# A gated mix of linear attention and a gated FFN: the first loads cut finer, and one transposed weight turned in two parts

## The chip, the cores and the metric

The kernel runs on one core of one Trainium2 chip. The metric is the device time of one execution in microseconds (us), lower being better; times of several executions are given by their median.

## The reference, cut to what matters

```
x = A_x                                   # [1, 2048, 640], bf16
g = sigmoid((x * gate_w).sum(-1))         # one gate for each token

# A: linear attention, H = 32 heads of Dh = 20
q, k, v = split(x @ wqkv)                 # wqkv [640, 1920]: columns q, k, v
pq = q @ w_phi (by head);  pk = k @ w_phi (by head)          # w_phi [32, 20, 20]
phi_q = [softmax(pq), softmax(-pq)];  phi_k = [softmax(pk), softmax(-pk)]
kv = phi_k^T v (by head, over all tokens);  z = sum of phi_k over tokens
o = (phi_q kv) / (phi_q z + 1e-6)
a = o @ wo

# B: gated FFN, F = 1728
b = (gelu(x @ w_gate) * (x @ w_up)) @ w_down

out = g * a + (1 - g) * b
```

## The kernel before, in words

The 2048 tokens are 16 tiles of 128 (`NT = 16`), in four blocks of four (`TB = 4`). The width D = 640 is five row blocks of 128 (`KD = 5`). `run` emits three parts in order: `loads`, `attention_state`, `ffn`. There is no loop on the chip: every instruction is written out by Python, and each engine runs its own in the order in which they were emitted. The small class `_Sched` keeps a semaphore for each engine and lanes of semaphores for each DMA queue; `sc.op` and `sc.dma` put a wait before an instruction for whatever wrote or still reads the buffers that it names. A buffer's key is the unit of such a wait: with the key `"wkT"` a reader waits for the whole tensor.

**Loads.** DMAs are issued on two queues, SyncE's (`"sp"`) and ScalarE's (`"act"`). The first x block is loaded as it lies, tokens on partitions, into `xtok`: two tiles on SyncE, two on ScalarE (`xload`, line 216). TensorE turns these four tiles itself (`x_transpose`, line 290), and VectorE (line 298) or ScalarE (line 296) copies the result to `xT`. ScalarE's queue then loads `w_phi` (line 229) and the gate vector (line 234); SyncE's loads the five row blocks of v's weight into `w3` (line 233, key `("wv", kt)`). After that SyncE issues transposing DMAs, in this order: x tiles 4 and 5, `wkT` (k's weight turned, line 220, one DMA for all five row blocks), x tiles 6 and 7, `wqT`, x tiles 8 to 11, x tiles 12 to 15 (x: line 224). The FFN's weights follow.

**State.** `attention_state` writes its order out by hand. TensorE begins with seven matmuls on a tensor of zeros (`warm(7)`, line 540), which VectorE fills first (line 536). Then come the four transposes of x, the v projection of tiles 0 to 3, row block by row block (`v_step`, line 363), and, interleaved, v projections of tiles 4 to 7 (`v_early`), the folds of `w_phi` into k's and q's weight (`fold`, line 331: row block kt of `wkT` or `wqT` times the block-diagonal `BD`, evacuated to `w3` or `wq2`), and k projections of tiles 0 to 3 (`k_early`, evacuated by exponentials on ScalarE, lines 413 and 416). The fragment of that order which later text refers to:

```
f(0,"k") f(1,"k") v_early(6) f(2,"k") f(3,"k") f(4,"k") v_early(7) k_early(0)
f(0,"q") f(1,"q") k_early(1) f(2,"q") f(3,"q") k_early(2) f(4,"q") k_early(3)
pq(0,1,1) pq(0,0,0) pq(0,3,3) gram(0) pq(0,2,2) ...
```

`pq(b, i, n)` computes one q feature block in PSUM bank 6 or 7 (by the parity of n); ScalarE reads it with two exponentials (line 518). `k_norm` normalises the k features on VectorE (lines 424, 428 and 433), and `gram` (line 449) adds phi_k^T v for one tile. All projections go through `mm`, whose matmul is line 351. Then the loop over tiles 4 to 15 repeats projection, normalisation, two `pq` and one `gram`.

**FFN.** `ffn` computes gate and up projections (line 351 again), the gelu (line 623) and the product (line 625), and the down projection together with the attention's output projection (line 708), block by block.

Of the kernel before, what the change touches and what calls it, by code (L numbers as in the profile page):

```python
# [3 lines left out]
P = 128  # L4
BF16 = mybir.dt.bfloat16
F32 = mybir.dt.float32
AF = mybir.ActivationFunctionType
# [100 lines left out]
class _Kernel:  # L108
    S, D, H, DH, F = 2048, 640, 32, 20, 1728
    KD = D // P  # L110
# [31 lines left out]
    def alloc(self):  # L142
        nc = self.nc
        S, D, KD, NT, BT, NFC, DH = self.S, self.D, self.KD, self.NT, self.BT, self.NFC, self.DH
        T = nc.alloc_sbuf_tensor
        self.xT = T("xT", [P, KD, S], BF16)
        self.wo_sb = T("wo_sb", [P, KD, D], BF16)
        self.wg_sb = T("wg_sb", [P, KD, 13 * P], BF16)
        self.wu_sb = T("wu_sb", [P, KD, 13 * P], BF16)
        self.wgu_sb = T("wgu_sb", [P, KD, P], BF16)  # L150
        self.wd_sb = T("wd_sb", [P, NFC, D], BF16)
        self.Eq = T("Eq", [P, 2, KD, S], BF16)
        self.KV = T("KV", [P, KD, 2, self.HB * self.DB], BF16)
        self.hmask = T("hmask", [P, 2, KD, self.HB], BF16)
        self.mask = T("mask", [P, KD, 8], BF16)
        self.ident = T("ident", [P, P], BF16)
        self.zero = T("zero", [P, 512], BF16)
        self.gz = T("gz", [P, P], BF16)
        self.gcol = T("gcol", [P, NT], F32)
        self.gtmp = T("gtmp", [P, NT], F32)  # L160
        self.Gm = T("Gm", [P, NT], F32)
        self.Gr = T("Gr", [P, NT], F32)
        self.BD = T("BD", [P, KD, 8 * DH], BF16)
        self.wphi_sb = T("wphi_sb", [P, KD, DH], BF16)

        def place(lists):
            size = {"b": 0}
            plans = []
            for items in lists:
                c = 0  # L170
                for name, shape, dt in items:
                    n = mybir.dt.size(dt)
                    for s_ in shape[1:]:
                        n *= s_
                    c = (c + 31) // 32 * 32
                    plans.append((name, shape, dt, c))
                    c += n
                size["b"] = max(size["b"], c)
            arena = T("arena%d" % len(self._arenas), [P, size["b"]], mybir.dt.uint8)
            self._arenas.append(arena)  # L180
            base = nc.lookup_mloc(arena).addr
            for name, shape, dt, c in plans:
                setattr(self, name, nc.alloc_sbuf_tensor_at(name, shape, dt, offset=base + c))
        self._arenas = []
        place([
            [("w3", [P, KD, 2 * D + 2], BF16), ("wq2", [P, KD, D], BF16)],
            [("hT0", [P, NFC, BT], BF16), ("gl", [P, 3, BT], BF16)],
        ])
        place([
            [("Ek", [P, self.NSE, 2, D], BF16), ("vaug", [P, self.NSV, self.H, self.DA], BF16),  # L190
             ("Dk", [P, self.NSE, 2, 2 * self.H], F32)],
            [("hT1", [P, NFC, BT], BF16)],
        ])
        place([
            [("xtok", [P, self.TB, D], BF16), ("wkT", [P, KD, D], BF16), ("wqT", [P, KD, D], BF16)],
            [("goT", [P, 8, KD, P], BF16), ("O1", [P, 2, D], BF16), ("O2", [P, 2, D], BF16),
             ("Og", [P, 2, D], BF16), ("RH", [P, 2, 8, 2, 16], F32), ("outsb", [P, 4, D], BF16)],
        ])
        self.ps = nc.alloc_psum_tensor("ps", [P, 4096], F32)
# [8 lines left out]
    def loads(self):  # L208
        sc, nc = self.sc, self.nc
        D, KD, DH, P_ = self.D, self.KD, self.DH, P  # L210
        w3 = self.wqkv.rearrange("(kt p) n -> p kt n", p=P)

        x4 = self.x[0:self.BT, :].rearrange("(p j) n -> p j n", j=self.TB)

        def xload(q, j):
            sc.dma(q, lambda e: e.dma_start(self.xtok[:, j:j + 2, :], x4[:, j:j + 2, :]),
                   writes=[("xtok", j), ("xtok", j + 1)])

        def wload(T, c0, key):
            sc.dma("sp", lambda e: e.dma_start_transpose(T[:, :, :], self.wqkv[:, c0:c0 + D]), writes=[key])  # L220

        def xturn(t, n):
            a, z = t * P, (t + n) * P
            sc.dma("sp", lambda e: e.dma_start_transpose(self.xT[:, :, a:z], self.x[a:z, :]),
                   writes=[("xT", k) for k in range(t, t + n)])
        sc.op("pool", lambda e: e.memset(self.gz[:, :], 0.0), writes=["gz"])
        xload("sp", 0)
        xload("act", 2)
        sc.dma("act", lambda e: e.dma_start(
            self.wphi_sb[:, :, :], self.wphi.rearrange("h d f -> (h d) f").rearrange("(i p) f -> p i f", p=P)),  # L230
            writes=["wphi"])
        for kt in range(KD):
            sc.dma("sp", lambda e: e.dma_start(self.w3[:, kt, 0:D], w3[:, kt, 2 * D:3 * D]), writes=[("wv", kt)])
        sc.dma("act", lambda e: e.dma_start(self.gz[0:KD, :], self.gw.rearrange("(k p) -> k p", p=P)), writes=["gz"])
        xturn(4, 2)
        wload(self.wkT, D, "wkT")
        xturn(6, 2)
        wload(self.wqT, 0, "wqT")
        xturn(8, 4)
        xturn(12, 4)  # L240
        half = 7 * P
# [10 lines left out]
        for r in (0, 1):  # L252
            sc.dma("sp", lambda e: e.dma_start(self.wd_sb[64 * r:64 * r + 64, 13, :], self.wd[13 * P:self.F, :]),
                   writes=[("wd13", r)])
        sc.dma("sp", lambda e: e.dma_start(self.wo_sb[:, :, :], self.wo.rearrange("(kt p) n -> p kt n", p=P)),
               writes=["wo"])
# [6 lines left out]
        for i in range(KD):  # L263
            n = self.HHI[i] - self.HLO[i] + 1
# [53 lines left out]
    def fold(self, kt, which, banks, ekey):  # L318
        sc = self.sc
        DH = self.DH  # L320
        wT = self.wkT if which == "k" else self.wqT
        for i in range(self.KD):
            lo, hi = self.HLO[i], self.HHI[i]
            for h in (0, 1):
                a, z = max(lo, 16 * h), min(hi, 16 * h + 15)
                if a > z:
                    continue
                n = (z - a + 1) * DH
                b, c0, k0 = banks[h], (a - 16 * h) * DH, (a - lo) * DH
                first, fin = (i == 0 or a == 16), (z in (15, 31) and i in (2, 4))  # L330
                sc.op("pe", lambda e: e.matmul(  # L331
                    self.bank(b)[:, c0:c0 + n], wT[:, i, kt * P:(kt + 1) * P], self.BD[:, i, k0:k0 + n],
                    start=first, stop=fin, skip_group_check=True),
                    reads=["w%sT" % which, ("BD", i)], writes=[("ps", b)], signal=fin)
        src = self.pair(banks)
        if which == "k":
            dst = self.w3[:, kt, self.D:2 * self.D].rearrange("p (b c) -> p b c", c=320)
        else:
            dst = self.wq2[:, kt, :].rearrange("p (i r c) -> p r i c", r=2, c=64)
            src = src.rearrange("p r (i c) -> p r i c", c=64)  # L340
        rd = [("ps", b) for b in banks]
        wr = [("w%s2" % which, kt)]
        if ekey == "d":
            self.sc.op("dve", lambda e: e.tensor_copy(dst, src), reads=rd, writes=wr)
        else:
            self.sc.op("act", lambda e: e.activation(dst, src, AF.Copy), reads=rd, writes=wr)
# [161 lines left out]
                      writes=[("KV", i, r, g)])  # L508
                self.kvk[i, r].append(("KV", i, r, g))

    def pq(self, b, i, n):
        sc = self.sc
        bank = 6 + n % 2
        for kt in range(self.KD):
            self.mm(bank, 0, 512, self.wq2[:, kt, i * P:(i + 1) * P], self.xT[:, kt, b * self.BT:(b + 1) * self.BT],
                    kt == 0, kt == self.KD - 1, [("xT", t) for t in range(4 * b, 4 * b + 4)] + [("wq2", kt)])
        for s, scale in ((0, 1.0), (1, -1.0)):
            sc.op("act", lambda e, s=s, scale=scale: e.activation(  # L518
                self.Eq[:, s, i, b * self.BT:(b + 1) * self.BT], self.bank(bank), AF.Exp, scale=scale),
                reads=[("ps", bank)], writes=[("Eq", b, s, i)])  # L520
# [11 lines left out]
    def attention_state(self):  # L532
        NT = self.NT
        order = [(b, i) for b in range(self.NB) for i in range(self.KD)]
        sc = self.sc
        sc.op("dve", lambda e: e.memset(self.zero[:, :], 0.0), writes=["zero"])

        def warm(n):
            for i in range(n):
                sc.op("pe", lambda e: e.matmul(self.bank(0), self.zero[:, 0:P], self.zero[:, :], start=True, stop=True),  # L540
                      reads=["zero"], writes=[("ps", 0)])
        vs, ve, xt = self.v_step, self.v_first_evac, self.x_transpose
        warm(7)
        xt(0, 6, "d")
        xt(1, 7, "a")
        xt(2, 2, "d")
        xt(3, 3, "a")
        for t in range(4):
            vs(t, 0)
        for t in range(4):  # L550
# [33 lines left out]
        self.k_norm(1)  # L584
        self.pq(0, 1, 1)
        self.pq(0, 0, 0)
        self.pq(0, 3, 3)
        self.columns = True
        self.gram(0)
        self.k_norm(2)  # L590
# [2 lines left out]
        n = 4  # L593
# [47 lines left out]
    def num(self, t):  # L641
        sc = self.sc
        NBK = self.NUMB
        DB, DH = self.DB, self.DH
        old = [("xtok", k) for k in range(4)] + ["wkT", "wqT"]
        w = self.HB * DB
        for i in range(self.KD):
            for s in (0, 1):
                for r in (0, 1):
                    bk, a, o0 = NBK + 2 * r + s, 64 * r, 3 * i * DB  # L650
# [4 lines left out]
                        signal=(i == self.KD - 1))  # L655
# [183 lines left out]
```

The softmax here doesn't subtract the row's maximum and nothing guards it: scores larger than these inputs give would overflow.

## Time and profile before

| what | value |
|---|---|
| median of 4 runs | 289.34 us (289.03 to 289.74) |
| profiled execution, time | 289.25 us |
| profiled execution, span | 288.0 us |
| TensorE busy (matmul) | 281.5 us, 98% of the span |
| TensorE weight loads | 190.0 us, 66% |
| VectorE busy | 166.7 us, 58% |
| ScalarE busy | 105.0 us, 36% |
| GpSimd busy | 27.6 us, 10% |
| issue to landing: `wkT`, `wqT` | 6.7 us, 8.6 us |
| issue to landing: v's row blocks, median of five | 4.7 us |
| ScalarE's table load | 1.28 us, from 2.46 us |

All times of the profile are counted from the start of the span; the execution takes 1.25 us more than the span. "PE" is TensorE's matmuls and "PEld" its weight loads, which run beside matmuls; DVE is VectorE, ACT is ScalarE, POOL is GpSimd, SPq is SyncE's queue of DMA issues. In the chain of waits each row is a start, a length and what the end of the kernel waited for during it. In a timeline each row is a start, a length, an engine, a line, an operation, and out<-in; a bracket at its end is the idle time before it and what ended that.

### The profile page before, as it was taken

How to read it: one execution, taken by the hardware profiler on the slowest of the kernel's cores; microseconds unless marked ns; L12 is line 12 of the kernel's file. 1: busy time of each engine (PE TensorE's matmuls, PEld its weight loads, DVE VectorE, ACT ScalarE, POOL GpSimd, SP SyncE). 2: the span in 40 equal slices, each digit the busy share in tenths (PEclk: the TensorE clock that was granted, in tenths of full speed). 3: DMA queues.
4: the chain of work that ended last, by engine and by line, in shares of the span. 5: the costliest groups of instructions: out<-in, count | busy, mean ns of one | idle time of the engine just before them, and what ended most of it. 6: DMA issues, size and time to landing. Idle time of an engine off the chain costs nothing.

```text
span 288.0 us, 7020 instructions
## 1 busy us (share of the span) xinstructions
PE 281.5 (98%) x3016; PEld 190.0 (66%) x3032; DVE 166.7 (58%) x337; ACT 105.0 (36%) x199; POOL 27.6 (10%) x52
## 2 busy tenths in 40 slices
PE   7999999999999999999999999999999999999996
PEld 3576689999994444444699744457764444777785
DVE  2248999999977552777776533227644232674001
ACT  3367887677663222222111332221133222022111
POOL 7000000000000000111113200001230000113000
PEclk9999999999999999999999999999999999999999
DMA  8999995000002000011112110000212000031211
GB/s 225 207 190 238 365 367 175 0 2 2 0 2 48 0 0 0 3 36 30 25 29 72 35 58 0 3 0 19 76 25 68 0 2 0 3 93 25 71 49 49
DMA packets 36938, 18.68 MB, mean 65 GB/s; under 512 B 28970, under 2 KB 36394, under 8 KB 36906
## 3 DMA queue, kind: packets, MB, share of 16 engines
q1 hardware_dynamic: 36096, 17.86, 24.7%
q8 instruction: 24, 0.39, 0.6%
q10 hardware_dynamic: 810, 0.35, 0.5%
q14 instruction: 8, 0.07, 0.1%
HBM read 9.04 MB, written 2.62 MB: 40 GB/s over the span
## 4 chain that ended last, share of the span: by engine, by line
PE 96%; DMA 1%; ACT 1%; issue 1%; ACTq 0%
PE ps L351 60%; PE ps L708 28%; PE ps L651 2%; PE ps L363 2%; PE ps L449 2%; DMA xtok<-in_A_x_dram 1%; PE ps L331 1%; ACT Ek L413 0%; PE ps L290 0%; ACT Eq L518 0%; ACT gl L631 0%; ACT outsb L721 0%; ACT gcol L416 0%; PE ps L313 0%; ACTq L42 0%
## 5 line engine op out<-in xcount | busy, mean ns | idle before, releaser
L625 DVE TENSOR_TENSOR hT<-ps,gl 128x512 bf16<-128x512 f32 x52 | 35.7, 690 | 55.2 <-PE ps L351 54.9
L708 PE MATMUL ps<-wd_sb,hT 64*128 64x320 bf16 (+2 forms) x918 | 67.5, 288 | 0.0
L351 PE MATMUL ps<-xT,wu_sb 128*128 128x512 bf16 (+1 forms) x266 | 64.0, 379 | 0.2
L351 PE MATMUL ps<-xT,wg_sb 128*128 128x512 bf16 (+1 forms) x261 | 62.9, 379 | 1.2 <-issue 1.0
L623 ACT ACTIVATE gl<-ps 128x512 bf16<-128x512 f32 x52 | 30.9, 597 | 71.5 <-PE ps L351 64.9
L708 PEld LDWEIGHTS ps<-wd_sb,hT 64*128 64x128 bf16 x918 | 46.6, 94 | 12.5 <-ACT gl L623 0.8
L351 PEld LDWEIGHTS ps<-xT,wu_sb 128*128 128x128 bf16 (+1 forms) x270 | 26.5, 99 | 29.7 <-DVE hT L625 0.4
L680 POOL TENSOR_TENSOR Og<-O,O 128x640 bf16<-128x640 bf16 x16 | 22.3, 1393 | 236.7 <-DVE O L678 236.7
L351 PEld LDWEIGHTS ps<-xT,wg_sb 128*128 128x128 bf16 (+1 forms) x270 | 25.9, 99 | 28.7 <-issue 0.5
L721 ACT ACTIVATE outsb<-ps,Gm 128x320 bf16<-128x320 f32 (+2 forms) x31 | 14.6, 515 | 74.8 <-PE ps L708 74.8
L351 PE MATMUL ps<-w,xT 128*64 128x512 bf16 (+6 forms) x398 | 41.6, 325 | 0.2
L351 PEld LDWEIGHTS ps<-w,xT 128*64 128x64 bf16 (+1 forms) x400 | 35.8, 107 | 4.8
L708 PE MATMUL ps<-wo_sb,goT 64*128 64x320 bf16 (+2 forms) x340 | 28.1, 288 | 0.0
L351 PE MATMUL ps<-xT,wq 128*64 128x512 bf16 (+1 forms) x184 | 26.1, 380 | 0.4 <-ACT Eq L518 0.3
L433 DVE TENSOR_TENSOR Ek<-Ek,Dk 128x640 bf16<-128x640 bf16 x32 | 25.0, 821 | 0.6
L678 DVE TENSOR_TENSOR O<-ps,RH 128x640 bf16<-128x640 f32 x32 | 24.7, 815 | 0.0
L424 DVE TENSOR_REDUCE Dk<-Ek 128x64 f32<-128x1280 bf16 x16 | 23.7, 1478 | 0.2 <-ACT gcol L416 0.2
L518 ACT ACTIVATE Eq<-ps 128x512 bf16<-128x512 f32 x40 | 21.7, 604 | 1.1 <-PE ps L351 0.8
L413 ACT ACTIVATE Ek<-ps 128x640 bf16<-128x640 f32 x32 | 20.7, 702 | 3.5 <-PE ps L351 3.5
L708 PEld LDWEIGHTS ps<-wo_sb,goT 64*128 64x128 bf16 x340 | 17.9, 94 | 4.5
L351 PEld LDWEIGHTS ps<-xT,wq 128*64 128x64 bf16 (+1 forms) x185 | 15.3, 108 | 3.5 <-ACT Eq L518 0.8
L667 DVE RECIPROCAL RH<-ps 128x32 f32<-128x32 f32 x16 | 5.7, 358 | 18.3 <-PE ps L651 18.2
(65 smaller groups left out, 148.8 us busy)
## 6 DMA issues: line engine op xcount, KB each, us to landing
out_dram<-outsb SPq DMA_DIRECT2D x7, 320.0 KB, 2.4
wd_sb<-in_B_w_down_dram SPq DMA_DIRECT2D x1, 2080.0 KB, 14.0
wg_sb<-in_B_w_gate_dram SPq DMA_DIRECT2D x1, 1120.0 KB, 6.1
wu_sb<-in_B_w_up_dram SPq DMA_DIRECT2D x1, 1120.0 KB, 8.6
wg_sb<-in_B_w_gate_dram SPq DMA_DIRECT2D x1, 960.0 KB, 9.6
wu_sb<-in_B_w_up_dram SPq DMA_DIRECT2D x1, 960.0 KB, 10.2
w<-in_A_wqkv_dram SPq DMA_DIRECT2D x5, 160.0 KB, 4.7
wo_sb<-in_A_wo_dram SPq DMA_DIRECT2D x1, 800.0 KB, 9.7
```

Of the source, the lines that this page charges most:

```text
L351: self.sc.op("pe", lambda e: e.matmul(self.ps[a:z, bank * 512 + c0:bank * 512 + c0 + n], lhs[:, a:z], rhs, start=first, stop=fin), reads=r ...
L363: sc.op("pe", lambda e, c0=c0, n=n, bk=bk, col=col: e.matmul(self.bank(bk)[:, col:col + n], self.xT[:, kt, t * P:(t + 1) * P], self.w3[:, ...
L413: self.sc.op("act", lambda e, s=s, scale=scale: e.activation(self.Ek[:, se, s, :], self.ps[:, o:o + self.D], AF.Exp, scale=scale), reads=[ ...
L424: sc.op("dve", lambda e: e.tensor_reduce(self.Dk[:, se, 0, :].rearrange("p (s h) -> p s h", h=H), self.Ek[:, se, :, :].rearrange("p s (h d ...
L433: sc.op("dve", lambda e, v=v, r=r: e.tensor_tensor(v, v, r, ALU.mult), reads=[("Rk", se)], writes=[("Ek", se, s)])
L518: sc.op("act", lambda e, s=s, scale=scale: e.activation(self.Eq[:, s, i, b * self.BT:(b + 1) * self.BT], self.bank(bank), AF.Exp, scale=sc ...
L623: sc.op("act", lambda e: e.activation(self.gl[:, slot, :], self.bank(banks[0]), AF.Gelu_apprx_tanh), reads=[("ps", banks[0])], writes=[("g ...
L625: sc.op("dve", lambda e: e.tensor_tensor(hT[:, c, :], self.bank(banks[1]), self.gl[:, slot, :], ALU.mult), reads=[("ps", banks[1]), ("gl", ...
L678: dve(lambda e, o=o, f=f, s=s: e.tensor_tensor(o, V[s][:, :, :, 0:DH], f, ALU.mult), rb + [key(6 + s)], [("O", s, sl)], guard=old)
L680: sc.op("pool", lambda e: e.tensor_tensor(self.Og[:, sl, :], self.O1[:, sl, :], self.O2[:, sl, :], ALU.add), reads=[("O", 0, sl), ("O", 1, ...
L708: sc.op("pe", lambda e: e.matmul(self.bank(bk, w), lhs, rhs, start=opens and x == 0, stop=end and not opens, skip_group_check=True), reads ...
L721: sc.op("act", lambda e: e.activation(dst, self.bank(bk, w), AF.Copy, scale=g), reads=rd, writes=wr)
```

## The change

- The first x block is loaded by four DMAs of one tile each, all on SyncE's queue.
- The five row blocks of v's weight come behind them: blocks 0 and 2 on ScalarE's queue, 1, 3 and 4 on SyncE's. `w_phi` and the gate vector stay on ScalarE's queue, behind v's two blocks.
- ScalarE's first action is one exponential on a constant, which loads the function table. It writes a column of `gtmp`, which is used again only by `gates`, much later.
- `wkT` is turned by two DMAs, row blocks 0 and 1, then 2 to 4, with x tiles 6 and 7 between them. `wqT` remains one DMA. The keys of both are by row block now.
- The warm-up uses a constant tensor of ones that is there before the kernel begins, instead of zeros written by VectorE; six matmuls instead of seven.
- x tile 3 is evacuated by VectorE instead of ScalarE.
- The third `pq` of block 0 uses PSUM bank 0 instead of bank 7.

```diff
-        self.zero = T("zero", [P, 512], BF16)
...
         def xload(q, j):
-            sc.dma(q, lambda e: e.dma_start(self.xtok[:, j:j + 2, :], x4[:, j:j + 2, :]),
-                   writes=[("xtok", j), ("xtok", j + 1)])
-
-        def wload(T, c0, key):
-            sc.dma("sp", lambda e: e.dma_start_transpose(T[:, :, :], self.wqkv[:, c0:c0 + D]), writes=[key])
+            sc.dma(q, lambda e: e.dma_start(self.xtok[:, j, :], x4[:, j, :]), writes=[("xtok", j)])
+
+        def vload(q, kt):
+            sc.dma(q, lambda e: e.dma_start(self.w3[:, kt, 0:D], w3[:, kt, 2 * D:3 * D]), writes=[("wv", kt)])
+
+        def wload(T, c0, key, a, z):
+            sc.dma("sp", lambda e: e.dma_start_transpose(T[:, :, a * P:z * P], self.wqkv[a * P:z * P, c0:c0 + D]),
+                   writes=[(key, k) for k in range(a, z)])
...
         sc.op("pool", lambda e: e.memset(self.gz[:, :], 0.0), writes=["gz"])
-        xload("sp", 0)
-        xload("act", 2)
+        sc.op("act", lambda e: e.activation(self.gtmp[:, 0:1], self.nc.const_aps.tensor(1.0, [P, 1], BF16), AF.Exp),
+              writes=["gtmp"])
+        for j in range(self.TB):
+            xload("sp", j)
+        for kt in range(KD):
+            vload("act" if kt in (0, 2) else "sp", kt)
         sc.dma("act", lambda e: e.dma_start(
             self.wphi_sb[:, :, :], self.wphi.rearrange("h d f -> (h d) f").rearrange("(i p) f -> p i f", p=P)),
             writes=["wphi"])
-        for kt in range(KD):
-            sc.dma("sp", lambda e: e.dma_start(self.w3[:, kt, 0:D], w3[:, kt, 2 * D:3 * D]), writes=[("wv", kt)])
         sc.dma("act", lambda e: e.dma_start(self.gz[0:KD, :], self.gw.rearrange("(k p) -> k p", p=P)), writes=["gz"])
         xturn(4, 2)
-        wload(self.wkT, D, "wkT")
+        wload(self.wkT, D, "wkT", 0, 2)
         xturn(6, 2)
-        wload(self.wqT, 0, "wqT")
+        wload(self.wkT, D, "wkT", 2, 5)
+        wload(self.wqT, 0, "wqT", 0, 5)
         xturn(8, 4)
         xturn(12, 4)
...
-                    reads=["w%sT" % which, ("BD", i)], writes=[("ps", b)], signal=fin)
+                    reads=[("w%sT" % which, kt), ("BD", i)], writes=[("ps", b)], signal=fin)
...
-    def pq(self, b, i, n):
-        sc = self.sc
-        bank = 6 + n % 2
+    def pq(self, b, i, n, bank=None):
+        sc = self.sc
+        bank = 6 + n % 2 if bank is None else bank
...
-        sc.op("dve", lambda e: e.memset(self.zero[:, :], 0.0), writes=["zero"])
-
-        def warm(n):
-            for i in range(n):
-                sc.op("pe", lambda e: e.matmul(self.bank(0), self.zero[:, 0:P], self.zero[:, :], start=True, stop=True),
-                      reads=["zero"], writes=[("ps", 0)])
+        ones = self.nc.const_aps.tensor(1.0, [P, 512], BF16)
+        for i in range(6):
+            sc.op("pe", lambda e: e.matmul(self.bank(0), ones[:, 0:P], ones, start=True, stop=True), writes=[("ps", 0)])
         vs, ve, xt = self.v_step, self.v_first_evac, self.x_transpose
-        warm(7)
         xt(0, 6, "d")
         xt(1, 7, "a")
         xt(2, 2, "d")
-        xt(3, 3, "a")
+        xt(3, 3, "d")
...
-        self.pq(0, 3, 3)
+        self.pq(0, 3, 3, 0)
```

More of the change, by code (lines that the diff above doesn't have):

```diff
@@ L644, in num @@
         DB, DH = self.DB, self.DH
-        old = [("xtok", k) for k in range(4)] + ["wkT", "wqT"]
+        old = [("xtok", k) for k in range(4)] + [(w, k) for w in ("wkT", "wqT") for k in range(self.KD)]
         w = self.HB * DB
```

## The prediction

> **What bounds the kernel now.** I read the page first, then the chain of waits in order of time, then the first 30 us on TensorE, on SyncE's queue and on the DMA engines.
>
> ```profile
> PE 281.5 (98%) x3016; PEld 190.0 (66%) x3032; DVE 166.7 (58%) x337; ACT 105.0 (36%) x199; POOL 27.6 (10%) x52
> ...
> PE 96%; DMA 1%; ACT 1%; issue 1%; ACTq 0%
> ```
>
> TensorE is busy 98% and carries 96% of the chain, so a microsecond saved ahead of it counts only if everything that it reads later is there a microsecond sooner. The chain of waits has two places where TensorE waits for another:
>
> ```profile
> 0.80 4.12 DMA xtok<-in_A_x_dram
> ...
> 4.96 1.29 PE ps L290 x20
> 6.25 4.56 PE ps L363 x32
> ...
> 20.49 0.63 PE ps L331 x12
> ...
> 27.61 0.99 ACT Eq L518 x2
> 28.60 0.05 issue
> 28.65 1.25 PE ps L351 x5
> ```
>
> The first is the x block (to 4.96), the second a wait for ScalarE's exponentials of line 518, after which line 351 starts at 28.65; the timeline gives TensorE 0.34 us idle there. The change goes at both. Whether the first gain lives is read from what TensorE needs next. Its weight loads in time, and SyncE's issues of the transposing DMAs:
>
> ```profile
> 15.21 1.36 PEld L351 LDWEIGHTS ps<-w,xT 128*128 128x128 bf16 x10
> 16.53 0.97 PEld L331 LDWEIGHTS ps<-BD,wkT 128*128 128x128 bf16 x18
> 17.59 2.62 PEld L351 LDWEIGHTS ps<-w,xT 128*128 128x128 bf16 x20
> 20.22 0.72 PEld L331 LDWEIGHTS ps<-BD,wqT 128*128 128x128 bf16 x12
> ```
>
> ```profile
> 3.76 2.27 SPq L224 DMA_TRANSPOSE xT<-in_A_x_dram  x1
> 6.08 3.81 SPq L220 DMA_TRANSPOSE wkT<-in_A_wqkv_dram  x1
> 9.93 1.41 SPq L224 DMA_TRANSPOSE xT<-in_A_x_dram  x1
> 11.38 4.96 SPq L220 DMA_TRANSPOSE wqT<-in_A_wqkv_dram  x1
> 16.38 7.35 SPq L224 DMA_TRANSPOSE xT<-in_A_x_dram  x2
> ```
>
> The answers on the tiles give the time to landing: 5.5 us for x tiles 4 and 5 (9.3), 6.7 for wkT (12.8), 5.2 for x tiles 6 and 7 (15.1), 8.6 for wqT: 11.38 + 8.6 = 19.98. The first load from wqT is at 20.22, and after x landed TensorE began 0.05 later (4.92, 4.96). So wqT has **0.19 us to spare**; x tiles 6 and 7 have none (15.1 against 15.21). Are those transposes themselves full? The DMA rate in slices of 0.1 us, from 12 and from 16 us:
>
> ```profile
> GB/s 195 151 92 90 56 54 143 243 248 95 253 289 284 292 244 233 220 212 195 31 61 49 67 164 36 23 10 51 72 41 56 236 241 195 23 131 136 261 287 289
> GB/s 284 287 287 287 300 289 289 289 292 292 294 289 435 269 269 269 91 61 85 26 3 28 10 8 8 8 10 10 10 8 10 10 266 287 289 289 118 287 292 294
> ```
>
> They move 289 GB/s in a rush, then drop nearly to nothing, then rush again: once at each change from one transposing DMA to the next. Time lost is the length of a dip less its bytes over 289 GB/s: 0.11 us at 8.9 (into wkT), 0.89 from 11.4 (into x 6 and 7), 1.24 from 13.9 (into wqT), 1.47 from 17.6, 1.39 from 21.4. Mean of the five 1.02.
>
> **The change part by part.** *Front.* Now 2 x 320 KB land at 4.7 and 4.92. Four 160 KB loads on SyncE are issued 0.49 apart (row of line 233: five in 2.44). Bytes begin at about 2.0; one tile at some 380 GB/s (2.5 to 4 us) is 0.43, and landing follows the bytes by about 0.5. Tiles land near 3.1, 3.6, 4.1, 4.6; if ScalarE's two v rows share the engines at once, about 1.0 MB is ahead of the last, 2.0 + 2.65 + 0.5 = 5.15. Then five transposes (0.056 each, 20 weight loads in 1.12) and the v steps start at 5.0 to 5.5, not 6.09. The wait for the last copies goes too: 16 steps at the 0.273 of the last four (1.09) are 4.36, not 4.56. Front gain 0.8 to 1.3; I take 1.1.
>
> *Cost of the front.* ScalarE's table (1.28) is already hidden, at 2.46; first, it delays v row 0 between 0 (the queue runs on) and 1.28. Row 0 is then issued at 0.8 to 2.1, landing by 4.1 to 4.8 more (v rows): 4.9 to 6.9. At worst the v steps start 0.8 late. wphi moves behind two v rows: 3.1 + 4.3 = 7.4, five products of 0.30 on VectorE end at 9.0, with the gate column (10.9) and the v evacuations (11.38) queued behind them: hidden. The gate vector's landing is not shown; between wphi's 4.3 and wqT's 8.6 from an issue near 3.6 it is there at 7.9 to 12.2, against 10.58, so it costs 0 to 1.6 before cover; I take 0, as wphi is its neighbour. VectorE's memset (0.27) goes; tile 3's copy takes 0.49 on VectorE, not 0.70 on ScalarE. All of this is ahead of the wqT wait below and covered by it; without that cover it counts in full.
>
> *Warm-up.* Six matmuls without a wait, at 0.42 each, from about 0.9 end at 3.4, as tiles arrive. The seven of before start from 1.25 to 3.78, and at 4.96 the rate has doubled (the granted clock reads 1.00 in every window and doesn't show it; the spacing does). If it doubles later, 20 transposes lose 20 x 0.05 = 1.0: 0 to 1.0, covered likewise. I take 0.
> The Trainium skill, TensorE: Matmul & The Clock Gate, Part 1, asks for about 3.4 us of sustained work in a free-running window before full rate; six matmuls are less than that, and by the page alone the 1.0 would be due.
>
> *SyncE's queue.* Seven copies (four x, three v) stand before the first transpose, now six: it is issued up to 0.48 later, or at no cost if it waits for the v bytes anyway, which are the same in total. I take 0.24.
>
> *wk in two parts.* Same bytes, one transposing DMA more ahead of wqT, so one more dip: 0.11 to 1.47, taken at the mean, 1.02. Below nothing is possible too, if shorter DMAs overlap better; against it, x 6 and 7, the short one, has dips of 0.89 and 1.24 on its two sides.
> The Trainium skill, DMA: Bandwidth & Descriptors, Rules for kernel authors, says that transfers under 64 KB are mostly overhead; both parts of wk (320 and 480 KB) are above it, so by the page the split is near free and the sum would be the second rival's.
>
> x tiles 6 and 7 come earlier (two blocks ahead of them, not five), so the v step at 15.21 is freed. The second part of wk is wanted at 16.53, less the gain 15.4. From 9.3 by landing intervals (2.35 for two blocks, from wkT's 12.8 to 15.1) it lands at 9.3 + 2.35 + 2.35 + 2.6 = 16.6: part of the gain is lost there already. wqT decides.
>
> *Sum at the first q fold.* wqT lands 1.02 + 0.24 = 1.26 later, at 21.24; less the 0.19 to spare, TensorE is **1.07 later** than now, with the whole front gain turned into waits. Then *bank 0 for the third q product*: banks 0 and 1 are free after line 416 (27.6), so the 0.34 idle goes (low end 0.28, by ten matmuls of 0.216 from 26.21); the following gram needs VectorE's products at 29.30 and would start at about 29.45: free. Net 1.07 - 0.34 = +0.73. The profiled execution took 289.25 (span 288.0 and 1.25 around it), so 289.98; it lies 0.09 under the median 289.34. I say **290.0**.
>
> **The rivals.** *Faster: transposes keep up.* If smaller pieces overlap and wqT lands at 18.9 or earlier, TensorE never waits for it: -1.1 - 0.34 = -1.45, 287.9; between, each microsecond is one. It becomes faster by over 0.2% (0.58 us, about what a measurement of this kernel can tell from no change) once wqT lands 0.05 earlier than now. For it: the dip into wkT was 0.11. Against: the other four.
> *No difference: the extra dip is like that into wkT.* wqT lands between 0.05 earlier and 1.1 later, net -0.58 to +0.57: 288.7 to 289.9. The front gain is then hidden behind wqT and the 0.34 pays for the rest.
> *The front doesn't come early* (v rows and x share the same engines): v steps at 6.1; with wqT late as forecast it changes nothing, 290.0.
>
> **How the numbers follow.** Forecast case, wqT at least 1.1 later: 0.58 (0.10 of it for the third rival, which ends at the same time). No difference: 0.24. Faster: 0.18. Ends: the costs at 1.47 + 0.48 give 1.95 - 0.19 - 0.28 = +1.48, 290.7 to 290.8; I add 0.1 for the median. The low end reaches through the second rival into the first, 288.4, leaving out most of the first and little else. The likeliest case alone: 289.9 to 290.8.
>
> **What would show it.** Five transposing issues ahead of the x tiles 8 on, with five dips between 8 and 20 us; wqT landing near 21.2; TensorE idle for 1 to 2.5 us in all before line 331's folds; v steps from 5.0 to 5.5; no idle at line 518's wait. I am wrong if wqT lands at or before 20.0, or if TensorE's time after 30 us changes.

## The result, and the profile after

The changed kernel takes 290.72 us (median of 44 runs, 289.32 to 293.11), the kernel before beside it 289.45 (63 runs, 288.51 to 290.68). The ratio is 1.0052, with a 95% interval of 1.0041 to 1.0063: 1.5 us slower (1.2 to 1.8). The spread is as telling as the median: 3.8 us, against 2.2 before. The profiled execution took 292.68 (span 291.4) and so belongs to the long ones; it shows the loss enlarged, 3.4 us of span where the medians differ by 1.3.

The page has the same make-up as before, with 3.3 us more on TensorE for the same work (one matmul fewer):

```profile
PE 284.8 (98%) x3015; PEld 191.2 (66%) x3031; DVE 166.8 (57%) x337; ACT 104.5 (36%) x199; POOL 27.6 (9%) x52
...
PE 96%; DMA 2%; issue 1%; SPq 0%; ACT 0%
```

The chain of waits of the changed kernel (start, length, what the end waited for; lines are 5 higher than before in this part):

```profile
2.20 4.86 DMA xtok<-in_A_x_dram
7.05 0.05 issue
7.10 0.71 PE ps L295 x5
7.82 6.95 PE ps L368 x32
...
15.96 2.66 PE ps L356 x19
...
24.36 0.63 PE ps L336 x12
...
28.34 0.32 PE ps L336 x6
...
30.07 3.19 PE ps L356 x14
33.26 0.00 issue
33.26 0.46 PE ps L454 x11
```

The x block now holds the chain to 7.05, not 4.92. The 32 matmuls of the first v steps take 6.95, not 4.56. The first q fold stands at 24.36, 3.87 later than before's 20.49, and nothing waits for a transposed weight anywhere between. The idle time ahead of the third q product is gone: from the last q fold (28.34; before 24.48) to the first gram (33.26; before 29.90) it is 4.92 us, not 5.42, so **bank 0 gives 0.50**. What remains, 3.36, is the whole difference of the spans: after 33 us the two kernels run alike.

TensorE's weight loads in time show both losses (the bracket is the idle time before a row and what ended it):

```profile
3.78 0.45 PEld L295 LDWEIGHTS ps<-ident,xtok 128*128 128x128 bf16 x5 [1.13 <-DMA xtok<-in_A_x_dram]
4.52 0.45 PEld L295 LDWEIGHTS ps<-ident,xtok 128*128 128x128 bf16 x5 [0.29 <-DMA xtok<-in_A_x_dram]
5.61 0.45 PEld L295 LDWEIGHTS ps<-ident,xtok 128*128 128x128 bf16 x5 [0.64 <-DMA xtok<-in_A_x_dram]
7.10 0.45 PEld L295 LDWEIGHTS ps<-ident,xtok 128*128 128x128 bf16 x5 [1.03 <-DMA xtok<-in_A_x_dram]
...
12.28 0.29 PEld L368 LDWEIGHTS ps<-w,xT 128*128 128x128 bf16 x2 [0.25 <-issue]
12.81 1.62 PEld L368 LDWEIGHTS ps<-w,xT 128*128 128x128 bf16 x12 [0.25 <-issue]
```

Four waits, one for each tile of x: they land at 3.74, 4.48, 5.57 and 7.06 (the trace records sixteen landing events for a tile, its shares; it has landed with the last of them). And the weight loads of two v matmuls take 0.53 us (12.28 to 12.81) until 12.8, then 0.27: TensorE ran at half rate until then. The granted-clock view reads 1.00 for every stretch; the trace also keeps a record of changes of the clock, which that view doesn't show: it begins with full rate at 12.98 here and at 4.62 in the kernel before.

SyncE's queue stands as predicted, with five transposing DMAs ahead of the x tiles from 8 on:

```profile
4.10 2.04 SPq L226 DMA_TRANSPOSE xT<-in_A_x_dram  x1
6.19 2.58 SPq L221 DMA_TRANSPOSE wkT<-in_A_wqkv_dram  x1
8.81 1.41 SPq L226 DMA_TRANSPOSE xT<-in_A_x_dram  x1
10.26 2.08 SPq L221 DMA_TRANSPOSE wkT<-in_A_wqkv_dram  x1
12.38 4.59 SPq L221 DMA_TRANSPOSE wqT<-in_A_wqkv_dram  x1
```

wqT takes 8.2 us from there and lands at 20.6. That is 0.6 later than before, but TensorE reads it at 24.09, 3.5 after it is there.

Two theories came out of this. *Clock*: the shorter warm-up with gaps behind it keeps TensorE at half rate. *Transfers*: the last piece of the x block comes late because other loads share the engines with it. The prediction's own reason, wqT's landing after one more transposing DMA, is the rival.

### The profile page after: what moved, and what is told of

Its sections match the earlier page's. It is cut to its first block, busy times and chain, and to the rows that moved or that the text cites. A ratio compares the mean times of both kernels' runs of the same rounds, so it can differ in the third digit from the quotient of the medians.

```text
span 291.4 us, 7028 instructions
## 1 busy us (share of the span) xinstructions
PE 284.8 (98%) x3015; PEld 191.2 (66%) x3031; DVE 166.8 (57%) x337; ACT 104.5 (36%) x199; POOL 27.6 (9%) x52
## 4 chain that ended last, share of the span: by engine, by line
PE 96%; DMA 2%; issue 1%; SPq 0%; ACT 0%
PE ps L356 60%; PE ps L709 28%; PE ps L368 3%; PE ps L652 2%; PE ps L454 2%; DMA xtok<-in_A_x_dram 2%; PE ps L336 1%; SPq L215 0%; PE ps L295 0%; ACT gl L632 0%; ACT outsb L722 0%; PE ps L318 0%
```

## The experiments

Each ratio is against the kernel before, run beside it, with its 95% interval.

### The clock

**The warm-up filled up** (e1_fill). The changed kernel, with warm-up matmuls in the gaps between the transposes:

```diff
-        for i in range(6):
-            sc.op("pe", lambda e: e.matmul(self.bank(0), ones[:, 0:P], ones, start=True, stop=True), writes=[("ps", 0)])
...
+        warm(7)
         xt(0, 6, "d")
+        warm(1)
         xt(1, 7, "a")
+        warm(2)
         xt(2, 2, "d")
+        warm(4)
         xt(3, 3, "d")
```

> After, with more warm-up matmuls so that TensorE has work while x lands: 7 ahead of the first transpose, 1, 2 and 4 more between the four tiles' transposes (6, 0, 0, 0 in after). Theory clock: in after TensorE's idle gaps during the x loads (0.23, 0.38 and 0.77 us) keep it at half rate, in the profiled execution until about 13 us, and that is most of the loss. Then the v steps (32 matmuls, 6.95 us in the profile of after) take 4.4 to 4.8, the spread between runs shrinks, and the median falls from 290.7 to 289.5 to 290.0, x still landing at 7. Theory wqT (that of the prediction): TensorE waits for wqT in any case, so the median stays at 290.4 to 290.9.

Measured: 289.75 (289.28 to 290.11), ratio 1.0013 (1.0003 to 1.0022). The spread falls from 3.8 to 0.8. Its weight loads, and its chain:

```profile
5.61 0.28 PEld L295 LDWEIGHTS ps<-ident,xtok 128*128 128x128 bf16 x5 [0.43 <-DMA xtok<-in_A_x_dram]
```

```profile
7.15 0.45 PE ps L295 x5
7.60 4.37 PE ps L368 x32
...
21.56 0.63 PE ps L336 x12
```

The third tile's transposes start at 5.61 in both kernels; their loads take 0.28 here and 0.45 there, and the v steps 4.37 against 6.95. Full rate is on record from 4.85. Nothing else moved: x still lands at 7.1. So the clock is worth 0.97 us by the two medians (1.1 by the two ratios), 2.8 in the two profiled executions (the first q fold at 21.56 and 24.36). That 21.56 is 1.07 later than before's 20.49 with full rate early in both: the price of the late x block, read from one execution of each kernel.

**The warm-up alone** (e6_warm6_only). The kernel before, with six matmuls on the constant ones:

```diff
-        sc.op("dve", lambda e: e.memset(self.zero[:, :], 0.0), writes=["zero"])
+        ones = self.nc.const_aps.tensor(1.0, [P, 512], BF16)
...
-        warm(7)
+        warm(6)
```

> Before, with only the warm-up of after: six matmuls on a constant, from 0.84, ending at 3.4, and then 1.5 us of idle until x lands at 4.9. Theory clock: the rate doubles later in most runs, so the median is 0.4 to 1.5 us slower than before and the slowest run lies above 291. Rival: six are enough, or the gap does no harm; the median is that of before within 0.2 us. Starting 0.4 earlier could also gain up to 0.2.

Measured: 290.68 (289.62 to 291.23), ratio 1.0038 (1.0025 to 1.0051): 1.1 us slower (0.7 to 1.5) with nothing else touched; 1.46 by the two medians. Its chain:

```profile
4.73 2.32 PE ps L289 x20
7.05 5.33 PE ps L362 x32
```

The 20 transposes take 2.32, not 1.29, and the v steps 5.33, not 4.56; full rate came at 8.86. The six matmuls, from 0.84, end near 3.6 and TensorE then has nothing to do until x lands at 4.7.

The Trainium skill, TensorE: Matmul & The Clock Gate, Part 1, says that full rate comes after about 3.4 us of sustained work, watched in windows that run free of the kernel, so that one kernel differs from run to run. These runs agree in the scatter. With six matmuls and gaps the profiled execution got full rate at 12.98 (the change), at 8.86 (e6) and, in runs shown below, at 9.02 (e2) and 4.37 (e9). With seven or more it came between 4.62 and 6.05 (before, e1, e5, e7, e8, e10 to e12); e4, with the warm-up of before, has no such record, and its transposes ran at half rate. In e3, below, with six, it came at 3.65, after 2.7 us of matmuls, which is less than the page's 3.4; from there the record changes in steps of 3.41.

### The transfers

**w_phi behind the v rows** (e9_wphi_last).

```diff
-        sc.dma("act", lambda e: e.dma_start(
+        sc.dma("sp", lambda e: e.dma_start(
             self.wphi_sb[:, :, :], ...
```

> After, with w_phi's load (640 pieces of 40 bytes) moved from ScalarE's queue to SyncE's, behind x and v; v rows 0 and 2 stay on ScalarE's queue. Theory w_phi: its small pieces hold up the engines in the middle of x, and one engine above all (the last tile's sixteen shares land between 5.70 and 7.06 in after); without them the last tile lands at 5.0 to 5.7, and the median falls to 289.6 to 290.2. Theory v rows: the two v rows alone keep the last tile at 6.3 or later and the median at 290.4 to 291.0. The clock may still miss, so the spread stays about 2 us or more.

Measured: 290.05 (288.53 to 290.86), ratio 1.0013 (0.9995 to 1.0030). The last tile lands at 5.83 instead of 7.06. In the changed kernel w_phi's 640 pieces of 40 bytes, on ScalarE's queue, run from 4.47 us, among the last tile's bytes, and the last tile's sixteen shares arrive from 5.70 to 7.06; here from 5.28 to 5.83. The DMA queues from 4.5 to 5.0 us (packets, MB, time of the packets as a share of that of 16 engines, which can pass 100%; q1 is SyncE's queue, q10 ScalarE's), in the changed kernel and then here:

```profile
q10 hardware_dynamic: 586, 0.02, 80.4%
q1 hardware_dynamic: 78, 0.08, 50.8%
```

```profile
q1 hardware_dynamic: 164, 0.19, 110.5%
```

So in this half microsecond SyncE's queue, with x on it, moves 0.08 MB beside the small pieces and 0.19 without them. At the 380 GB/s of the prediction the missing 0.11 MB is 0.3 us (an estimate); the rest of the 1.2 goes with the uneven arrival of the shares (1.36 apart against 0.55), whose cause is not shown. The runs fall in two groups, 288.5 to 289.4 and 289.8 to 290.9, which fits the warm-up that is still the short one. The profiled execution is the shortest, with full rate from 4.37, and in it a weight has become late:

```profile
16.63 0.94 PEld L336 LDWEIGHTS ps<-BD,wkT 128*128 128x128 bf16 x18 [0.26 <-DMA wkT<-in_A_wqkv_dram]
```

**All v rows behind x, on SyncE's queue** (e2_v_behind).

```diff
-            vload("act" if kt in (0, 2) else "sp", kt)
+            vload("sp", kt)
```

> After, with all five v rows on SyncE behind the four x tiles, none on ScalarE. Theory sharing: in after the last x tile lands at 7.06 because the two v rows and w_phi on ScalarE's queue take the DMA engines at the same time; here it lands at 4.6 to 5.3 and the v steps start at 5.0 to 5.6 (7.6 in after); median 288.6 to 289.8. Rival, small loads: 160 KB tiles on one queue are slow by themselves; the last tile still lands after 6.3 and the median stays above 290.2. Theory wqT: x lands early, but TensorE then waits for wqT before line 336's q folds, which cannot start before 20.7; median 289.5 to 290.2.

Measured: 289.80 (288.97 to 290.83), ratio 1.0014 (0.9999 to 1.0028). The last tile lands at 6.07, between the two expectations: a miss of the experiment, for ScalarE's queue, freed of the v rows, now begins with w_phi, whose pieces run at 2.3 to 3.2. It takes a neighbour away and puts another one earlier. Full rate came at 9.02, so the time has the clock's loss in it too. The third tile landed at 5.68, and the fourth while the third was being turned:

```profile
5.73 0.99 PEld L295 LDWEIGHTS ps<-ident,xtok 128*128 128x128 bf16 x10 [1.24 <-DMA xtok<-in_A_x_dram]
```

**Single tiles in the kernel before** (e7_tiles_two_queues), on the two queues in turn (`xload` loads one tile), all else as before:

```diff
-        xload("sp", 0)
-        xload("act", 2)
+        xload("sp", 0)
+        xload("act", 1)
+        xload("sp", 2)
+        xload("act", 3)
```

> Before, with the x block in four loads of one tile, alternately on SyncE's and ScalarE's queue; nothing else moved. If loads of one tile are slow by themselves, the last tile lands after 5.3 (4.9 before) and the run is slower. If it is what shares the engines with them (v rows, w_phi's 640 pieces of 40 bytes), the last lands at 4.7 to 5.0, the first near 3.5, and the time is that of before within 0.3 us: the first tiles' transposes run earlier and fill the idle time, but the last tile sets the start of the v steps.

Measured: 289.71 (289.00 to 290.11), ratio 1.0012 (0.9999 to 1.0026). The last tile lands at 4.81, no earlier than the pairs do (4.59 to 4.92 in before, e4, e5, e6 and e8, which load them alike), and the next wait is there at once, for x tiles 6 and 7:

```profile
15.64 1.36 PEld L352 LDWEIGHTS ps<-w,xT 128*128 128x128 bf16 x10 [0.45 <-DMA xT<-in_A_x_dram]
```

### The parts by themselves

**wk in one part** (e3_wk_whole), in the changed kernel.

```diff
-        wload(self.wkT, D, "wkT", 0, 2)
+        wload(self.wkT, D, "wkT", 0, 5)
         xturn(6, 2)
-        wload(self.wkT, D, "wkT", 2, 5)
```

> After, with wkT turned by one DMA again, x tiles 6 and 7 behind it. Theory wqT: wqT lands 0.6 to 1.2 earlier than in after and the median falls by as much, to 289.5 to 290.1. Theories clock and sharing: in after TensorE reaches the q folds at 21.4 or later, behind wqT's 20.6, so the split costs nothing and the median stays at 290.4 to 291.0.

Measured: 291.34 (288.86 to 292.58), ratio 1.0056 (1.0029 to 1.0083). No gain from undoing the split: wqT lands at 20.4, only 0.15 earlier, far ahead of its reader (22.83). With the spread of these ten runs the intervals leave room for some 0.8 us either way. The clock's record of its profile is instructive: full from 3.65, half again from 7.06, full from 10.48. The v steps, at half rate for their first 2.7 us, take 5.77.

**The split alone** (e5_split_only): the kernel before with wkT in two DMAs and the keys by row block.

```diff
-        wload(self.wkT, D, "wkT")
+        wload(self.wkT, D, "wkT", 0, 2)
         xturn(6, 2)
-        wload(self.wqT, 0, "wqT")
+        wload(self.wkT, D, "wkT", 2, 5)
+        wload(self.wqT, 0, "wqT", 0, 5)
```

> Before, with only wkT turned in two parts (the order of after: blocks 0 and 1, x tiles 6 and 7, blocks 2 to 4, wqT). The prediction's term: wqT lands 1.02 later (0.11 to 1.47), 20.1 to 21.4 where TensorE began by 5.0, so the q folds wait and the run is 0.3 to 1.2 us slower than before. Rival, from the trace of after (issue of wqT one microsecond later than before, landing 0.6 later, of which 0.4 are the v rows): the split costs 0 to 0.3 us at wqT and the time is that of before within 0.2 us, or 0.1 faster, as x tiles 6 and 7 come sooner.

Measured: 289.56 (288.90 to 290.02), ratio 1.0002 (0.9990 to 1.0014): 0.06 us slower, at most 0.40 (the median beside it is 289.22, 0.34 lower). TensorE's waits for both weights are there in the profile, and the q fold is late by half of what was predicted:

```profile
17.00 0.94 PEld L333 LDWEIGHTS ps<-BD,wkT 128*128 128x128 bf16 x18 [0.32 <-DMA wkT<-in_A_wqkv_dram]
...
20.76 0.62 PEld L333 LDWEIGHTS ps<-BD,wqT 128*128 128x128 bf16 x12 [0.20 <-DMA wqT<-in_A_wqkv_dram]
```

wqT lands at 20.72, 0.74 later than in before's profile, and the q fold starts 0.54 later. The profiled execution, 289.82, is 0.26 above its own median, so that half of this may be its own. And one profile of each can't size the split: with the loads of before unaltered, wqT landed at 18.97 (e4), 18.98 (e6), 19.98 (before) and 20.05 (e8), a spread of 1.1.

**Bank 0 alone** (e4_bank0).

```diff
-        self.pq(0, 3, 3)
+        self.pq(0, 3, 3, 0)
```

> Before, with only the third q product moved to PSUM bank 0. All theories: the 0.34 us idle of TensorE at 28.3 goes and nothing else moves: 0.25 to 0.35 us faster than before, ratio 0.9988 to 0.9991. If the idle comes back later (ScalarE's exponentials late for the following products), ratio 1.000.

Measured: 288.93 (288.07 to 289.25), ratio 0.9979 (0.9965 to 0.9992): 0.6 us faster (0.2 to 1.0). The three q products run through:

```profile
21.00 0.63 PE ps L331 x12
...
24.99 0.32 PE ps L331 x6
...
26.72 3.19 PE ps L351 x14
29.90 0.01 issue
29.91 0.46 PE ps L449 x11
```

From the last q fold to the gram it is 4.92, exactly as in the changed kernel; 0.50 gained, of which the idle time was 0.34. Its profiled execution is as long as before's all the same (span 288.0): its transposes ran at half rate, 2.12 against 1.29, and the first q fold is at 21.00. So before's profile, with 20.49, shows one of that kernel's quicker starts.

### Versions put together

**Bank 0 and a full warm-up, in the kernel before** (e8_fill_bank0): nine matmuls on the constant ones, none of the other parts.

```diff
-        warm(7)
+        warm(9)
...
-        self.pq(0, 3, 3)
+        self.pq(0, 3, 3, 0)
```

> Before, with bank 0 for the third q product and nine warm-up matmuls on the constant from 0.84 to 4.7, so that TensorE is busy until x lands; loads as before. Theory clock: a busy stretch without a gap from 0.84 on doubles the rate no later than in before, so the runs are those of bank 0 alone or up to 0.3 us better: ratio 0.9970 to 0.9988 to before, spread under 1.2 us. If the gap of before did no harm, the ratio is that of bank 0 alone, 0.998.

Measured: 288.52 (287.92 to 289.05), ratio 0.9961 (0.9946 to 0.9976): **1.1 us faster than the kernel before, the lowest ratio of all** (its interval overlaps those of e4, e10 and e11). Its chain has no wait for a transfer:

```profile
0.84 4.00 PE ps L539 x9
4.84 1.44 PE ps L289 x20
6.27 4.56 PE ps L362 x32
...
20.42 0.63 PE ps L330 x12
...
26.14 3.19 PE ps L350 x14
```

**w_phi last and a full warm-up, in the changed kernel** (e10_wphi_last_fill): e9's edit, and warm-up matmuls 7, 0, 1, 0 ahead of the four transposes.

```diff
-        sc.dma("act", lambda e: e.dma_start(
+        sc.dma("sp", lambda e: e.dma_start(
             self.wphi_sb[:, :, :], ...
...
+        warm(7)
         xt(0, 6, "d")
+        warm(0)
         xt(1, 7, "a")
+        warm(1)
         xt(2, 2, "d")
```

> After, with both suspected causes taken away: w_phi's load behind x and v on SyncE's queue (last x tile at 5.8) and warm-up matmuls 7, 0, 1, 0 around the transposes. If w_phi's place and the clock are the whole of the loss, the slow half of the run with w_phi last (290.3 to 290.9) goes and the median is 288.5 to 288.9, as its fast half, 0.2 to 0.3% faster than before. If a third cause remains, the median stays above 289.2.

Measured: 289.22 (288.61 to 289.69), ratio 0.9981 (0.9966 to 0.9995). The last tile lands at 5.80 (e1, with the same kind of warm-up and w_phi where the change has it: 7.10). With both causes treated, the 1.5 us are gone and some more, and a third thing comes up:

```profile
17.22 0.94 PEld L336 LDWEIGHTS ps<-BD,wkT 128*128 128x128 bf16 x18 [0.74 <-DMA wkT<-in_A_wqkv_dram]
```

**x on two queues, v and w_phi behind it** (e11_two_queues): as e10, with the tiles of x in turn on the two queues, all v rows on SyncE's, warm-up of seven.

```diff
-            xload("sp", j)
+            xload(("sp", "act")[j % 2], j)
...
-            vload("act" if kt in (0, 2) else "sp", kt)
+            vload("sp", kt)
```

> As the run with w_phi last and the fill, but the four x tiles alternate between SyncE's and ScalarE's queue and all five v rows follow on SyncE's: last x tile at 4.8 instead of 5.8, warm-up 7. If the front is now the limit, this is 0.5 to 1.0 us faster than that run. If the transposed weights are (second part of wkT at 16.6 to 17.0, wqT at 20.2 to 20.7), TensorE waits for them and the time is the same within 0.2 us: about 288.6 to 288.9.

Measured: 288.83 (288.49 to 289.17), ratio 0.9977 (0.9962 to 0.9992). The last tile lands at 4.74, no earlier than the pairs of before, but about half of the 20 transposes are done by then (their weight loads run from 3.70 without a pause), and the v steps' weight loads start at 5.72, not 6.04: here is the early front that the change was to bring.

```profile
5.72 4.25 PEld L368 LDWEIGHTS ps<-w,xT 128*128 128x128 bf16 x32
...
14.58 1.41 PEld L356 LDWEIGHTS ps<-w,xT 128*128 128x128 bf16 x10
16.64 0.94 PEld L336 LDWEIGHTS ps<-BD,wkT 128*128 128x128 bf16 x18 [0.66 <-DMA wkT<-in_A_wqkv_dram]
...
20.21 0.71 PEld L336 LDWEIGHTS ps<-BD,wqT 128*128 128x128 bf16 x12
```

The v step for tile 6 is at 14.58, 0.63 earlier than before's 15.21, and the wait of 0.66 for wkT's second part takes that back: the q fold loads at 20.21, in the kernel before at 20.22. The gain that is left is bank 0's.

**The same with wk in one part** (e12_two_queues_whole): e3's edit on e11.

> As e11, with wkT turned by one DMA ahead of x tiles 6 and 7. Then TensorE waits for x tiles 6 and 7 (15.2 in before) rather than for the second part of wkT; wqT lands near 20.0. If the split helps an early front, this is slower than e11 by 0.1 to 0.5 us; if it only moves the wait, the same within 0.2 us; if one DMA fewer is worth what the prediction said, faster by 0.3 to 0.7.

Measured: 289.85 (289.06 to 290.61), ratio 1.0007 (0.9991 to 1.0023), 1.0 above e11 by the medians and 0.9 by the ratios, more than the 0.1 to 0.5 that was expected if the split helps:

```profile
16.78 1.36 PEld L355 LDWEIGHTS ps<-w,xT 128*128 128x128 bf16 x10 [1.96 <-DMA xT<-in_A_x_dram]
```

Without the split TensorE waits 1.96 for x tiles 6 and 7; with an early front the split saves about 1 us, though wqT lands no later with it (20.12 in e11, 20.33 here). (Why they come at 16.7 here, and at 15.1 in the kernel before with wk in one part too, was not told apart: w_phi's and the v rows' places differ as well.)

The Trainium skill, DMA: Bandwidth & Descriptors, Issuing engines are not separate DMA queues, says that transfers issued by different engines run on the same 16 DMA engines and interleave. The landings of the last x tile agree: 7.06 and 7.10 with v rows and w_phi on the other queue, 5.83 and 5.80 with the v rows alone, 4.74 with x first on both queues.

## Why the prediction was right and wrong

It said 290.0, slower by 0.55 to 0.73; it was slower by 1.3 in the medians and 1.5 by the ratio. The direction held, and of the reasons given for it only parts.

- **"Front gain 0.8 to 1.3; I take 1.1"**: the step that failed first, with the wrong sign. It expected tiles near 3.1, 3.6, 4.1, 4.6, the last at 5.15 at worst; they landed at 3.74, 4.48, 5.57, 7.06. The sum counted bytes over the rate of big transfers and took 0.5 for landing. It left out w_phi's 640 small pieces, which stood in ScalarE's queue behind two v rows and which the prediction looked at only for their own reader. Moving them takes 1.2 to 1.3 off the landing (7.06 to 5.83, 7.10 to 5.80); one queue with v rows beside it has 1.1 more (5.80 to 4.74). Without the clock the late front costs 1.07 at the first q fold (e1). Whether it is the number of pieces or any load in that place that does it was not varied.
- **"0 to 1.0, covered likewise. I take 0"** (the warm-up): the price was in the range, the cover was not there. The clock costs 0.97 by the medians and 1.1 by the ratios in the changed kernel (e1), and 1.1 by the ratio alone (e6). The cover was TensorE's wait for wqT; with a front that is late rather than early there is no such wait. The sentence on the clock's page had the 1.0 as due, and about that much was lost; the size is luck, as the 1.0 was for the 20 transposes alone, and in the profiled execution most of the loss is in the v steps (6.95 against 4.56).
- **wk in two parts, "taken at the mean, 1.02"**: mis-sized. It moved the time by 0.06, at most 0.40 (e5), where the sum had 1.02 less 0.19. With the split, wqT landed 0.74 later in one pair of profiles (e5 and before), 0.15 later in another (the changed kernel and e3) and 0.21 earlier in a third (e11 and e12), within the 1.1 by which it moves with the loads unaltered; so its own effect on the landing stays open. The mean of five dips was no estimate for one more of them. The "0.19 us to spare" was one execution's figure too: in e4, with the same loads, it was 1.76. The page on DMAs that was set against it, by which the split is near free, came closer on the time.
- **"1.07 later" at the first q fold**: by another cause, 1.07 without the clock and 3.87 in the profiled execution. Its agreement with e1's figure is accident.
- **"Net 1.07 - 0.34 = +0.73"**: bank 0 gave 0.50 from the last q fold to the gram in the profile of every kernel that has it, 0.16 more than the idle time. The next gram did start without a wait, as said.
- **What held**: the table load did not delay the DMA issues; the idle time at line 518's wait went; time after 33 us is unchanged; wqT landed at 20.6, between the two marks of 20.0 and 21.2; wkT's second part, put at 16.6, is read at 16.63 and 16.64 as soon as it lands where the front is early (e9, e11; at 17.22 in e10). Neither of its two signs of being wrong showed, though the path was wrong: the marks that failed were the v steps, from 7.61 and not 5.0 to 5.5, and TensorE's wait of 1 to 2.5 us ahead of the folds, of which there was none. The claim that an early front is turned into a wait for transposed weights is shown by e11, in wkT rather than wqT.
- **The rivals**: "the front doesn't come early" was nearest, but was priced at v steps from 6.1, not 7.61, and its time depended on the wqT wait that did not come.

The sum in measured sizes: late front +1.07 (e1), clock +0.97, bank 0 -0.50, together +1.54, against 1.5 by the ratio. That is closer than the parts allow, for the 1.07 is from single executions and the 0.97 from medians. By the ratios alone, e1, which has the late front and bank 0, is 0.4 slower than before, which with bank 0 at 0.50 leaves 0.9 for the late front; and e10, whose last tile lands 1.3 earlier than e1's, is 0.9 faster than e1.

Open: how the 1.1 us between 5.80 and 4.74 divide between the second queue for x and the absence of v rows beside it, since e11 changed both; and what makes the pauses between transposing DMAs. Why e4's 0.6 and e8's 1.1 exceed bank 0's 0.50 is argued only: e4's interval holds 0.50, e8's ends at 0.7, and e8's longer warm-up should spare it some of the longer runs of the kernel before.

## What to carry to other kernels

A kernel's start is set by the last piece of its first load, so look at everything else that is on the DMA engines at that moment (here a load of 640 tiny pieces on another queue), and put it behind. Let a warm-up last until the data arrives: here six matmuls and the gaps behind them cost about 1 us, and filling the gaps brought it back; when it fails, the spread of the times shows it as well as the median. Before a cost is called covered, compare when the covering transfer lands with when its reader will come, also for the case that another step of the sum fails.

## What was not expected of the hardware

- The table load, 0.80 to 2.08 us on ScalarE, did not hold up that engine's DMA issues: the two v rows were issued from 0.86 and w_phi at 1.77, while it ran.
- The granted-clock view said 1.00 throughout while matmuls ran at half rate until 12.8 us; the spacing of like matmuls, 0.53 against 0.27 for two, tells it, and so does the trace's record of changes of the clock.
- Full rate, once there, can be lost again in the first microseconds: in its profiled execution e3 had it at 3.65, lost it at 7.06 and had it back at 10.48.
- A load is as late as the last of its sixteen shares: those of the last x tile arrived over 1.36 us (5.70 to 7.06).
